# Linear attention with a feed-forward block: `num` bank by bank, and weight preparation, word loads and spills written in another order

## The chip, the cores and the metric

The kernel runs on one core of a Trainium2 chip. The metric is the device time of one execution in microseconds (us). A core has five engines, each of which works strictly in its own written order: PE (TensorE, matmuls and transposes; its weight loads are listed apart as PEld), DVE (VectorE), ACT (ScalarE), POOL (GpSimd) and SP (SyncE, which here issues all the DMAs).

## The reference, cut to what matters

```python
def phi(x):                                  # x: 8 x 8 x 576 x 64, w_phi: 64 x 128
    proj = einsum('bhsd,df->bhsf', x, w_phi)
    proj = proj - max(abs(proj), axis=-1, keepdims=True)
    return concatenate([exp(proj), exp(-proj)], axis=-1)
q_p, k_p = phi(q), phi(k)
kv  = einsum('bhsf,bhsd->bhfd', k_p, v)
z   = sum(k_p, axis=2)
num = einsum('bhsf,bhfd->bhsd', q_p, kv)
den = einsum('bhsf,bhf->bhs', q_p, z)[..., None] + 1e-06
x = (num / den).transpose(0, 2, 1, 3).reshape(4608, 512)
h = x @ w_in                                 # 512 x 2048
g = h * tanh(log1p(exp(h)))
out = g @ w_out                              # 2048 x 512
```

## The kernel before, in words

**Two stages.** The first 280 us or so are the attention stage, all the rest the feed-forward stage (`h` L580, `o` L709 and L732). The feed-forward products run in a split of seven block products, with each fp32 number as a high and a low fp32r part.

**A step of the attention stage.** The 4608 tokens and the heads are cut into 36 units n (NU = 36) of 512 columns. Keys run LEAD = 4 units ahead of queries. In step n PE does, in this order: `dt_n` (L449, sixteen transposes of the centred queries), `pp_k` (L300, projection of the keys of unit n+5), `pp_q` with `xt` (L309 and L315, the next projection of queries, with the transposes of the finished x of the unit before between its matmuls), `num_n` (L340 in `q_num`, 64 matmuls into two PSUM banks i = 0 and 1), `kvps` (L340 in `k_sum`, the product of keys and values), and then `dt_(n+1)`.

**Who waits for whom.** `dt`, `xt`, `num` and `kvps` share four PSUM buffers (pool `ps_b`), which they take in turn. So the second half of `xt` waits until ACT has read the first `dt` bank (`e_q`, exp, L454), the first bank of `num` waits for the exps of the second, the second bank of `num` waits until ACT has copied `xt` (`xs`, L501), and the next `dt` waits until DVE has read the `num` banks (`x`, L482). DVE's work in a step is `m_k` (L331) and `e_k` (L332), `m_q` (L429), `r` (L479), `x` (L482, twice) and `e_q` (L435), all on the step's own data. ACT's is `e_q` (L454, four), `xs` (L501, two), `e_k` (L374, two), `r` (L474, two) and `kv` (L406).

**Weight preparation.** Meanwhile the weights, which arrive as words of 64 bits, are made into their high and low parts, in pieces; 16 of these, called beat pieces, lie in the attention stage, one in two steps. Piece i is counted from 0: pieces 0, 1, 2, 3 are (in,0,0), (in,0,1), (in,1,0), (in,1,1). A piece consists of: the load of its words (SP, L168), `absolute` (ACT, L187), `clamp` (POOL, L190), `shift` (DVE, L194), `sign` (DVE, L198), `scale` (DVE, L204), `low_scale` (POOL, L213), `low` (POOL, L219), `total` (POOL, L231), four `sums` (POOL, L242), `hi` (ACT, CAST, L247), `lo` (POOL, L251), and from piece 4 of the inner matrix on two stores, the spills (SP, L271), of which the second carries what `lo` wrote. Their DVE operations read and write SBUF; those of the step, named above, read PSUM.

**What sets the order.** Every operation is put into one list by `at(time, function)` with a planned time: `base(n)` is the planned start of step n, to which hand-tuned offsets are added (`BEAT_AT` for a beat piece, `LOAD_AT`, `K_AT`, `Q_AT`, `EXP_AT`). The list sorted by time is the written order of all engines. A planned time is only a place in that order; what runs when is decided by the waits.

The constants at the top, BEAT_AT among them, give for a beat piece the offsets of `absolute, clamp, shift, sign, scale, low_scale` from its own step; with that line the diff begins.

Of the kernel before, what the change touches and what calls it, by code (L numbers as in the profile page):

```python
# [27 lines left out]
NU = NTOK * NHP // 512  # L28
# [3 lines left out]
LEAD = 4  # L32
LEAD_STEP = 3.04
L_AT = (0.0, 2.62, 3.19, 7.71, 9.38)
STEP = 7.341
# [3 lines left out]
SPILL_AT = (1.2, 1.9)  # L39
# [7 lines left out]
EXP_AT, MAX_AT = 2.95, 2.5  # L47
# [2 lines left out]
PRE = (11.72, 6.53)  # L50
CONV = (13.41, 14.719)
WORD_AT = 4.79
BEAT_AT = (-5.73, -5.54, -4.04, -4.03, 3.3, 0.5)
BEAT_LOW, BEAT_HI = 3.4, 16.43
X0_AT = (38.06, 20.0)
X0_STORE_AT = (16.4, 16.35, 16.3, 16.25, 16.2, 15.0, 14.9)
# [32 lines left out]
def attention_then_mish(ctx, tc, qT, kT, va, w_phi, w_in, w_out, w_out2, out):  # L89
# [81 lines left out]
    def weight_ops(kind, fp, k, quiet, early):  # L171
# [104 lines left out]
        if early:  # L276
            ops = list(zip(BEAT_AT, (absolute, clamp, shift, sign, scale, low_scale)))
        elif not quiet:
# [57 lines left out]
    def halves(ps, lhsT, rhs, start, stop):  # L336

        for h in range(2):
            rows = slice(h * D, (h + 1) * D)
            nc.tensor.matmul(ps[rows], lhsT[:, rows], rhs[h], start=start, stop=stop, skip_group_check=True)  # L340
# [115 lines left out]
    def q_num(n):  # L456
        c, g = divmod(n, 2)
        es = q_live.pop(n)
        x = x_live[n] = att.tile([P, 2, 2, P], F32, tag="x", name=f"x_{n}", bufs=3)
        for i in range(2):  # L460
            num_live[n, i] = ps_b.tile([P, 2, 2, VW], F32, tag="b", name=f"num{i}_{n}")
        for j in range(2):
            for i in range(2):
                for t in range(2):
                    r0 = (2 * c + t) * P
                    for s in range(2):
                        halves(num_live[n, i][:, t, j], es[:, j, s, (2 * i + t) * P:(2 * i + t + 1) * P],
                               [kv[(r0 + h * D) // S, 2 * g + i][:, j, s] for h in range(2)],
                               start=(t == j == s == 0), stop=(s == 1))
# [363 lines left out]
    def at(time, fn, *args):  # L833
        events.append((time, len(events), fn, args))

    def base(step):
        if step < 0:
            return step * LEAD_STEP
        return min(step, NU - LEAD) * STEP + max(0, step - NU + LEAD) * TAIL_STEP

    for u in range(NU):
        t, after = base(u - LEAD), base(u - LEAD + 1)
        a = K_AT if u >= LEAD else L_AT
        if u < LEAD:
            t = after = base(-LEAD) + u * LEAD_STEP
        at(t + (LOAD_AT[0] if u >= LEAD else -11.1), k_load, u)
        at(t + (LOAD_AT[1] if u > LEAD else V_AT[u]), v_load, u)
        at(t + a[0] - (1.7 if u == LEAD + 1 else 0.0), k_proj, u)
        at(t + a[1], k_center, u)
        if u < LEAD:  # L850
            at(t + a[2], k_exps, u)
        else:
            at(t + EXP_AT, k_exp, u, 1)
            at(t + a[2], k_exp, u, 0)
        at(after + a[3], k_sum, u)
        at(after + a[4], k_store, u)
        t, after, end = base(u), base(u + 1), base(u + 2)
        cut = STEP - TAIL_STEP
        after -= cut if u == NU - LEAD - 1 else 0.0
        close_by = end - (cut if u >= NU - LEAD - 2 else 0.0)  # L860
        if u >= NU - LEAD:
            after = end = close_by = t
        a = T_AT if u >= NU - LEAD else Q_AT
        early = 0.49 if u == 1 else 0.0
        at(t + LOAD_AT[2] - early, q_load, u)
        if 3 <= u <= NU - LEAD:
            at(t + a[0], q_proj_out, u, u - 3)
        else:
            at(t + a[0] - early, q_proj, u)
        if 3 <= u < NU - LEAD:  # L870
            at(t + MAX_AT, q_max, u)
            at(t + a[1], q_sub, u)
        else:
            at(t + a[1] - early, q_center, u)
        for j in range(2):
            at(after + a[2] + 0.45 * j - early, q_turn, u, j)
            shift = (0.0, -0.8)[j] if u == NU - LEAD - 1 else (0.8, 0.0)[j] if u == NU - LEAD else 0.0
            at(after + a[3] + 1.2 * j - early + shift, q_exp, u, j)
        at(end + a[4], q_num, u)
        at(end + a[5], q_den, u)  # L880
        at(end + a[5] + 0.05, q_norm, u)
        if u > NU - LEAD - 3:
            at(close_by + a[6] + (1.78 if u in (NU - LEAD - 2, NU - LEAD - 1) else 0.0), q_out, u)
        at(close_by + a[7] + (0.9 if u == NU - 1 else -0.68 if u == NU - LEAD - 2 else 0.0), q_store, u)
# [26 lines left out]
    def t_of(n):  # L911
        if n > first2:
            m = n - first2
            return t_of(first2) + m * FF2STEP + max(0, (m - 2) // NSEC) * TRAIL
        return begin + 5.6 + (n - AHEAD) * FFSTEP if n >= AHEAD else begin - PRE[0] + PRE[1] * n

    quiet_at = [(3, 0), (4, 0), (6, 0)] + [(n, w) for n in range(9, first2 - 3, 3) for w in (0, 1)]
    quiet_at += [(first2 - 3, 0), (first2 - 3, 2), (first2 - 2, 3)]
    for i, pc in enumerate(pieces):
        quiet = i >= EARLY  # L920
        if quiet:
            n, which = quiet_at[i - EARLY]
            clock = t_of(n) + BITS_AT[which]
            load_at = clock - WORDS_AT
        else:
            clock = CONV[0] + CONV[1] * i - WORD_AT
            load_at = clock + WORD_AT + (LOAD_AT[3] if i else -12.0)
        beat = 2 <= i < EARLY
        bits, sums, high, spill = weight_ops(*pc, quiet, beat)
        if beat:  # L930
            clock = base(2 * i)
            load_at = clock + BEAT_AT[0] - 11.0
        at(load_at, weight_load, *pc)
        for delay, op in bits:
            wait = base(2 * i + 1) + Q_AT[1] + 0.02 if i < 2 and delay > 1.0 else 0.0
            at(max(clock + delay * (0.85 if quiet else 1.0), wait - (0.49 if i == 0 else 0.0)), op)
        clock += LOW_AT[which] if quiet else BEAT_LOW if beat else WORD_AT
        for j, (cost, op) in enumerate(sums):
            if beat:
                clock = base(2 * i) + (BEAT_HI + 0.1 * (j - high) if j >= high else BEAT_LOW + 0.1 * j)  # L940
            at(clock, op)
            if pc[1] >= 2 and j in (high, len(sums) - 1):
                at(clock + (SPILL_AT[j > high and not quiet] if not beat else 1.2 if j == high else 3.2), spill, int(j > high))
            clock += cost

    for s, (sc, fps) in enumerate(segs):
# [7 lines left out]
        t = t_of(n - 2) - XS_EARLY if n >= AHEAD + 2 else begin - X0_AT[s]  # L954
# [12 lines left out]
    for n, (s, sc, fp, first, last) in enumerate(steps):  # L967
        t = t_of(n)
        if second(n):
            a, m = STEP2_AT, n - first2  # L970
# [4 lines left out]
            if n == len(steps) - 1:  # L975
                a = a[:4] + tuple(x - LAST for x in a[4:])
# [23 lines left out]
            if last:  # L1000
                t5, a = t_of(n + 2), DRAIN_AT
# [12 lines left out]
        a = STEP1_AT  # L1014
# [92 lines left out]
```

## Time and profile before

| | us |
|---|---|
| median of 3 runs | 1021.59 (1021.11 to 1024.95) |
| the profiled execution | 1026.97 |
| span of its profile | 1025.2 |
| PE busy | 999.5 (97%) |
| DVE, ACT, POOL busy | 750.0, 505.0, 284.0 |

The profile is of one execution. PE is busy nearly throughout; its share is an average over the two stages, and the rows below take them apart. "Idle before" in a row is the time in which the engine did nothing just ahead of that row, with what ended it; "issue" means that it waited for nothing that the profile shows. PEclk is the granted clock of TensorE, 1.00 being 2.4 GHz and 0.50 the lower level of 1.2 GHz.

### The profile page before, as it was taken

The page shows a single profiled execution, that of the slowest core. Times are in us where ns is not written, and L with a number is a line of the kernel's source. Part 1 is how long each engine was busy: PE and PEld are TensorE (multiplying, and loading weights), DVE is VectorE, ACT ScalarE, POOL GpSimd, SP SyncE. Part 2 cuts the span into 40 slices and gives each one's busy share as a digit, 9 for nine tenths or more (in the row PEclk, how much of TensorE's full clock was granted, in tenths as well). Part 3 has the DMA queues.
Part 4 walks back from the last instruction along what each step waited for, and adds up shares of the span by engine and source line. Part 5 has one row for each costly group of instructions (what it writes and reads, how often), then busy time and mean ns, then how long its engine had stood idle before and what let it go on. Part 6 is the DMA issues. An engine that isn't in the chain of part 4 may idle for free.

```text
span 1025.2 us, 28984 instructions
## 1 busy us (share of the span) xinstructions
PE 999.5 (97%) x12418; PEld 957.4 (93%) x12418; DVE 750.0 (73%) x1168; ACT 505.0 (49%) x904; POOL 284.0 (28%) x267
## 2 busy tenths in 40 slices
PE   8879999999999999999999999999999999999998
PEld 7879988999899999999999999999999999999998
DVE  7769878988755878979886576767676767575755
ACT  5657877877753545544544442423232333333332
POOL 0554354536424314654347001000000001010101
PEclk9989999999999999999999999999999999999999
DMA  6536557776499777898849895959595959585842
GB/s 212 182 127 208 177 172 257 237 249 188 144 355 396 293 275 258 265 362 321 283 156 346 304 359 207 343 190 347 191 355 183 349 195 332 210 315 216 309 162 75
DMA packets 111200, 259.02 MB, mean 253 GB/s; under 512 B 8672, under 2 KB 47328, under 8 KB 109024
## 3 DMA queue, kind: packets, MB, share of 16 engines
q1 hardware_dynamic: 111072, 257.17, 70.9%
q8 instruction: 98, 1.61, 0.6%
q14 instruction: 30, 0.25, 0.1%
HBM read 179.27 MB, written 77.86 MB: 251 GB/s over the span
## 4 chain that ended last, share of the span: by engine, by line
PE 91%; ACT 4%; issue 2%; DMA 1%; POOL 1%; DVE 0%; SPq 0%; ACTq 0%
PE h L580 35%; PE o L732 22%; PE o L709 14%; PE num L340 7%; PE kvps L340 7%; ACT e_q L454 4%; PE dt L449 2%; PE pp_k L300 2%; PE pp_q L309 1%; PE pp_q L300 0%; DMA kraw<-kT 0%; DMA qraw<-qT 0%; DMA v<-va 0%; ACT w_out L187 0%; PE xt L315 0%
## 5 line engine op out<-in xcount | busy, mean ns | idle before, releaser
L580 PE MATMUL h<-xc,win 128*128 128x256 f32 x3024 | 380.4, 283 | 0.0
L580 PEld LDWEIGHTS h<-xc,win 128*128 128x128 f32 x3024 | 373.8, 192 | 4.5
L804 POOL TENSOR_TENSOR part<-part,du 128x512 f32<-128x512 f32 x18 | 23.3, 1293 | 425.7 <-DVE du L794 425.7
L732 PE MATMUL o<-wa,gh 128*128 128x256 f32 x720 | 130.7, 283 | 0.0
L732 PEld LDWEIGHTS o<-wa,gh 128*128 128x128 f32 x720 | 111.8, 192 | 0.0
L709 PE MATMUL o<-wout,gh 128*128 128x512 f32 x432 | 108.2, 392 | 0.0
L732 PE MATMUL o<-wa,gl 128*128 128x256 f32 x360 | 100.7, 283 | 0.0
L612 DVE TENSOR_TENSOR u<-h,u 128x512 f32<-128x512 f32 x72 | 49.5, 687 | 69.3 <-PE h L580 69.3
L732 PE MATMUL o<-wb,held 128*128 128x256 f32 x795 | 95.8, 281 | 0.2 <-DVE du L794 0.2
L732 PEld LDWEIGHTS o<-wb,held 128*128 128x128 f32 x795 | 94.9, 189 | 0.4 <-DVE du L794 0.4
L709 PEld LDWEIGHTS o<-wout,gh 128*128 128x128 f32 x432 | 77.7, 189 | 13.9
L340 PE MATMUL num<-kv,e_q 128*64 128x65 f32 x2304 | 81.2, 226 | 5.7 <-issue 2.2
L340 PEld LDWEIGHTS num<-kv,e_q 128*64 128x64 f32 x2304 | 74.0, 139 | 13.1 <-ACT e_q L454 5.8
L454 ACT ACTIVATE e_q<-dt 128x512 f32<-128x512 f32 x144 | 74.3, 604 | 18.7 <-PE dt L449 18.6
L340 PE MATMUL kvps<-v,e_k 128*64 128x65 f32 (+1 forms) x2560 | 78.6, 224 | 2.5 <-issue 2.5
L340 PEld LDWEIGHTS kvps<-v,e_k 128*64 128x64 f32 (+1 forms) x2560 | 73.5, 138 | 4.7 <-issue 3.0
L628 ACT ACTIVATE sb<-h 128x256 f32<-128x256 f32 x45 | 17.3, 385 | 119.3 <-PE h L580 85.5
L374 ACT ACTIVATE e_k<-e_k 128x1024 f32<-128x1024 f32 x64 | 67.6, 1057 | 14.2 <-DVE e_k L332 14.0
L631 ACT ACTIVATE u<-u 128x768 f32<-128x768 f32 x45 | 38.1, 847 | 72.8 <-DVE u L612 72.8
L667 ACT CAST gh<-sb 128x1024 fp32r<-128x1024 f32 x45 | 47.2, 1049 | 50.4 <-DVE sb L660 50.4
L732 PEld LDWEIGHTS o<-wa,gl 128*128 128x128 f32 x360 | 68.6, 192 | 0.0
L679 DVE TENSOR_TENSOR gl<-sb,gh 128x1024 fp32r<-128x1024 f32 x45 | 61.0, 1355 | 0.7 <-ACT gh L667 0.7
(111 smaller groups left out, 1612.5 us busy)
## 6 DMA issues: line engine op xcount, KB each, us to landing
win<-in_spill SPq DMA_DIRECT2D x44, 896.0 KB, 8.2
xc<-xc_spill SPq DMA_DIRECT2D x63, 512.0 KB, 5.7
xc_spill<-xc SPq DMA_DIRECT2D x56, 512.0 KB, 6.5
wa<-out_spill SPq DMA_DIRECT2D x29, 768.0 KB, 5.8
in_spill<-wst_in SPq DMA_DIRECT2D x24, 448.0 KB, 3.3
v<-va SPq DMA_DIRECT2D x32, 325.0 KB, 4.4
qraw<-qT SPq DMA_DIRECT2D x36, 256.0 KB, 3.6
x_spill<-xs SPq DMA_DIRECT2D x36, 256.0 KB, 2.3
```

The lines of the kernel that those rows point to most:

```text
L300: nc.tensor.matmul(ps[:, j, n], src, w_phi2[rows], start=True, stop=True)
L340: nc.tensor.matmul(ps[rows], lhsT[:, rows], rhs[h], start=start, stop=stop, skip_group_check=True)
L374: nc.scalar.activation(e[:, :, s], e[:, :, 0], AF.Exp, scale=2.0 * s - 1.0)
L454: nc.scalar.activation(e[:, s, h], ps, AF.Exp, scale=2.0 * s - 1.0)
L580: nc.tensor.matmul(ps, w, x, start=(i in (0, 2) and m == 0), stop=(m == 5), skip_group_check=True)
L612: nc.vector.tensor_tensor(u[:, 0:3:2] if second(n) else u[:, 1:3], hy, u2.unsqueeze(1).broadcast_to([P, 2, CH]), op=ALU.add)
L631: nc.scalar.activation(u[:, 0:3], u[:, 0:3], AF.Mish)
L667: nc.scalar.copy(gh, u_live[n][4])
L679: nc.vector.tensor_tensor(gl, u_live[n][4], g_live[n]["h"].bitcast(F32), op=ALU.subtract)
L709: nc.tensor.matmul(o_live[s][tt], g[:, 2 * f + which, cols], wout[fp][:, f, k], start=(first and g is gh and f == k == 0), stop=(last and ...
L732: nc.tensor.matmul(ps, g, w, start=(start and k == 0), stop=(stop and k == 2), skip_group_check=True)
L804: nc.gpsimd.tensor_tensor(cross, cross, d_live[s, tau][0].unsqueeze(1).broadcast_to([P, 2, CH]), op=ALU.add)
```

## The change

It has seven parts.

1. `absolute` of a beat piece gets a place 0.12 later in the plan, by which it stands behind the two `xs` copies of its step on ACT.
2. `q_num` writes all 32 matmuls of bank 0 ahead of the 32 of bank 1; before, the banks took turns of 16.
3. For units 5 to 8 of the keys the two `e_k` exps stand together behind the two `r`; before, one stood ahead of them.
4. In the last unit of the keys, `k_sum` and `k_store` stand ahead of that step's `num` and `r`.
5. The load of a beat piece's words gets a later place on SP, behind the load of `v`.
6. Of piece 2, `shift` and `sign` go one step (7.341) later, and `scale`, `low_scale`, `low`, `total` and `sums` behind those of piece 1.
7. The second spill of a beat piece goes from 3.2 to 5.25 behind its place in the plan, which is behind the loads of `qraw` and `v` on SP.

```diff
-BEAT_AT = (-5.73, -5.54, -4.04, -4.03, 3.3, 0.5)
+BEAT_AT = (-5.61, -5.54, -4.04, -4.03, 3.3, 0.5)
...
-        for j in range(2):
-            for i in range(2):
+        for i in range(2):
+            for j in range(2):
                 for t in range(2):
...
         else:
-            at(t + EXP_AT, k_exp, u, 1)
+            at(t + (EXP_AT if u > LEAD + 4 else a[2]), k_exp, u, 1)
             at(t + a[2], k_exp, u, 0)
-        at(after + a[3], k_sum, u)
-        at(after + a[4], k_store, u)
+        at(after + a[3] - (1.34 if u == NU - 1 else 0.0), k_sum, u)
+        at(after + a[4] - (1.7 if u == NU - 1 else 0.0), k_store, u)
...
+    def bits_of(bits, *which):
+        return [bits[k][1] for k in which]
+
...
             clock = base(2 * i)
-            load_at = clock + BEAT_AT[0] - 11.0
+            load_at = clock - (15.0 if i > 3 else 13.4)
         at(load_at, weight_load, *pc)
         for delay, op in bits:
+            if i == 2 and op in bits_of(bits, 2, 3):
+                delay += STEP
+            if i == 2 and op in bits_of(bits, 4):
+                delay += 0.05
+            if i == 2 and op in bits_of(bits, 5):
+                delay += 6.2
...
-                clock = base(2 * i) + (BEAT_HI + 0.1 * (j - high) if j >= high else BEAT_LOW + 0.1 * j)
+                clock = base(2 * i) + (BEAT_HI + 0.1 * (j - high) if j >= high else BEAT_LOW + 0.1 * j + (3.35 if i == 2 else 0.0))
             at(clock, op)
             if pc[1] >= 2 and j in (high, len(sums) - 1):
-                at(clock + (SPILL_AT[j > high and not quiet] if not beat else 1.2 if j == high else 3.2), spill, int(j > high))
+                at(clock + (SPILL_AT[j > high and not quiet] if not beat else 1.2 if j == high else 5.25), spill, int(j > high))
```

**POOL in steps 1 to 4.** In the rows, `w_in_1` and `t_in_1` with the lower numbers belong to piece 1, `w_in_0` and `t_in_0` to piece 2; `w_in_1_1089` is piece 3. `L213` is `low_scale`, `L219` `low`, `L231` `total`, `L242` `sums`, `L251` `lo`, `L190` `clamp`. Before:

```order
L213 TENSOR_SCALAR w_in_1_736<-words_in_1_585 128x512
L219 TENSOR_TENSOR t_in_1_855<-w_in_1_736,t_in_1_855 128x512
L213 TENSOR_SCALAR w_in_0_757<-words_in_0_548 128x512
L231 TENSOR_TENSOR w_in_1_736<-w_in_1_736,t_in_1_855 128x512
L242 TENSOR_TENSOR w_in_1_736<-w_in_1_736 128x128 x2
L219 TENSOR_TENSOR t_in_0_1014<-w_in_0_757,t_in_0_1014 128x512
L231 TENSOR_TENSOR w_in_0_757<-w_in_0_757,t_in_0_1014 128x512
L242 TENSOR_TENSOR w_in_0_757<-w_in_0_757 128x128 x2
L242 TENSOR_TENSOR w_in_1_736<-w_in_1_736 128x128
L242 TENSOR_TENSOR w_in_0_757<-w_in_0_757 128x128 x2
L242 TENSOR_TENSOR w_in_1_736<-w_in_1_736 128x128
L251 TENSOR_TENSOR win_697<-w_in_1_736,win_697 128x896
```

After:

```order
L213 TENSOR_SCALAR w_in_1_736<-words_in_1_583 128x512
L219 TENSOR_TENSOR t_in_1_853<-w_in_1_736,t_in_1_853 128x512
L231 TENSOR_TENSOR w_in_1_736<-w_in_1_736,t_in_1_853 128x512
L242 TENSOR_TENSOR w_in_1_736<-w_in_1_736 128x128 x4
L251 TENSOR_TENSOR win_697<-w_in_1_736,win_697 128x896
L213 TENSOR_SCALAR w_in_0_761<-words_in_0_586 128x512
L219 TENSOR_TENSOR t_in_0_1012<-w_in_0_761,t_in_0_1012 128x512
L231 TENSOR_TENSOR w_in_0_761<-w_in_0_761,t_in_0_1012 128x512
L242 TENSOR_TENSOR w_in_0_761<-w_in_0_761 128x128 x4
L190 TENSOR_SCALAR w_in_1_1089<-w_in_1_1089 128x512
L213 TENSOR_SCALAR w_in_1_1089<-words_in_1_893 128x512
L251 TENSOR_TENSOR win_1242<-w_in_0_761,win_1242 128x896
```

Piece 1 is finished, `lo` included, before piece 2's `low_scale` begins, and piece 3's `clamp` and `low_scale` come right behind piece 2's sums.

**DVE in steps 1 to 3.** `L194` is `shift`, `L198` `sign`, `L204` `scale`; the other lines are the step's own. Before:

```order
L194 TENSOR_SCALAR w_in_1_736<-w_in_1_736 128x512
L194 TENSOR_SCALAR w_in_0_757<-w_in_0_757 128x512
L198 SCALAR_TENSOR_TENSOR w_in_0_757<-words_in_0_548,w_in_0_757 128x512
L198 SCALAR_TENSOR_TENSOR w_in_1_736<-words_in_1_585,w_in_1_736 128x512
L204 TENSOR_SCALAR t_in_1_855<-w_in_1_736 128x512
L331 TENSOR_REDUCE m_k_957<-pp_k_883 128x8
L332 TENSOR_TENSOR e_k_956<-pp_k_883,m_k_957 128x2x512
L429 TENSOR_REDUCE m_q_961<-pp_q_900 128x8
L479 RECIPROCAL r_964<-r_964 128x8
L482 TENSOR_TENSOR x_921<-num_2_922,r_964 128x256
L482 TENSOR_TENSOR x_921<-num_2_923,r_964 128x256
L435 TENSOR_TENSOR e_q_1012<-pp_q_900,m_q_961 128x2x512
```

After, from piece 1's `scale` on:

```order
L204 TENSOR_SCALAR t_in_1_853<-w_in_1_736 128x512
L331 TENSOR_REDUCE m_k_954<-pp_k_879 128x8
L332 TENSOR_TENSOR e_k_953<-pp_k_879,m_k_954 128x2x512
L429 TENSOR_REDUCE m_q_958<-pp_q_897 128x8
L479 RECIPROCAL r_960<-r_960 128x8
L482 TENSOR_TENSOR x_918<-num_2_919,r_960 128x256
L482 TENSOR_TENSOR x_918<-num_2_920,r_960 128x256
L435 TENSOR_TENSOR e_q_1008<-pp_q_897,m_q_958 128x2x512
L194 TENSOR_SCALAR w_in_0_761<-w_in_0_761 128x512
L198 SCALAR_TENSOR_TENSOR w_in_0_761<-words_in_0_586,w_in_0_761 128x512
L204 TENSOR_SCALAR t_in_0_1012<-w_in_0_761 128x512
```

Piece 2's `shift` and `sign` have left the place ahead of piece 1's `scale` and stand one step later, between `e_q` and the next `m_k`, with piece 2's `scale`, which stood there before, behind them.

**ACT in step 1**, from the exps of `dt_1` to the copy of `kv`. Before:

```order
L187 ACTIVATE w_in_1_736<-words_in_1_585 128x512
L187 ACTIVATE w_in_0_757<-words_in_0_548 128x512
L501 COPY xs_759<-xt_0_738 128x4x64
L501 COPY xs_759<-xt_0_739 128x4x64
L374 ACTIVATE e_k_799<-e_k_799 128x2x512
L474 ACTIVATE r_807<-num_1_765 128x4
L474 ACTIVATE r_807<-num_1_766 128x4
```

After:

```order
L187 ACTIVATE w_in_1_736<-words_in_1_583 128x512
L501 COPY xs_757<-xt_0_738 128x4x64
L501 COPY xs_757<-xt_0_739 128x4x64
L187 ACTIVATE w_in_0_761<-words_in_0_586 128x512
L474 ACTIVATE r_806<-num_1_765 128x4
L474 ACTIVATE r_806<-num_1_766 128x4
L374 ACTIVATE e_k_799<-e_k_799 128x2x512 x2
```

Piece 2's `absolute` went behind the `xs` copies, and the first `e_k` exp went behind the two `r`.

## Rows read from the trace of the kernel before

**Rows 1.** Windows: us, then busy us of PE, PEld, DVE, ACT, POOL; PEclk, DMA share, GB/s

```profile
40.00:60.00 20.00, 13.40 (x364) 12.67 (x364) 15.53 (x22) 9.76 (x21) 13.40 (x17) 0.94 0.38 124
...
280.00:300.00 20.00, 20.00 (x225) 18.55 (x222) 10.02 (x19) 11.76 (x23) 7.08 (x6) 1.00 0.88 323
```

**Rows 2.** Waits of PE: who waited for what, us in total, times, longest

```profile
PE xt L315 <- ACT e_q L454: 6.8, 2, 5.9
...
PE num L340 <- ACT xs L501: 0.7, 2, 0.6
```

**Rows 3.** PE, timeline: start, us, engine, line, operation, count [idle before]

```profile
39.01 0.69 PE L340 MATMUL num<-kv,e_q 128*64 128x65 f32 x16
...
43.70 0.71 PE L449 MATMUL dt<-ident,e_q 64*128 64x64 f32 x16
...
51.33 1.01 PE L449 MATMUL dt<-ident,e_q 64*128 64x64 f32 x16 [0.62 <-DVE x L482]
...
60.39 0.69 PE L315 MATMUL xt<-ident,x 64*128 64x64 f32 x4 [5.94 <-ACT e_q L454]
61.36 3.63 PE L340 MATMUL num<-kv,e_q 128*64 128x65 f32 x64 [0.29 <-ACT e_q L454]
...
66.80 0.71 PE L449 MATMUL dt<-ident,e_q 64*128 64x64 f32 x16
...
69.57 2.09 PE L340 MATMUL num<-kv,e_q 128*64 128x65 f32 x64
...
73.45 0.71 PE L449 MATMUL dt<-ident,e_q 64*128 64x64 f32 x16
```

**Rows 4.** ACT, timeline, the stretch of PE's longest wait

```profile
58.41 0.94 ACT L247 CAST win<-w_in 128x896 fp32r<-128x896 f32 x1 [6.77 <-POOL w_in L242]
```

**Rows 5.** POOL, timeline, pieces 1 to 3

```profile
46.96 1.28 POOL L219 TENSOR_TENSOR t_in<-w_in,t_in 128x512 f32<-128x512 f32 x1 [4.09 <-DVE t_in L204]
48.33 1.55 POOL L213 TENSOR_SCALAR w_in<-words_in 128x512 f32<-128x512 uint32 x1
...
53.06 1.27 POOL L219 TENSOR_TENSOR t_in<-w_in,t_in 128x512 f32<-128x512 f32 x1 [0.76 <-DVE t_in L204]
54.41 1.26 POOL L231 TENSOR_TENSOR w_in<-w_in,t_in 128x512 f32<-128x512 f32 x1
55.75 2.63 POOL L242 TENSOR_TENSOR w_in<-w_in 128x128 f32<-128x128 f32 x6
59.43 2.08 POOL L251 TENSOR_TENSOR win<-w_in,win 128x896 fp32r<-128x896 f32 x1 [1.05 <-ACT win L247]
62.30 0.61 POOL L190 TENSOR_SCALAR w_in<-w_in 128x512 f32<-128x512 f32 x1 [0.79 <-ACT w_in L187]
```

**Rows 6.** DVE, timeline, pieces 1 to 3 between the step's own work

```profile
46.39 0.43 DVE L204 TENSOR_SCALAR t_in<-w_in 128x512 uint32<-128x512 uint32 x1
...
52.56 0.42 DVE L204 TENSOR_SCALAR t_in<-w_in 128x512 uint32<-128x512 uint32 x1
...
67.37 0.42 DVE L194 TENSOR_SCALAR w_in<-w_in 128x512 uint32<-128x512 uint32 x1
...
68.50 1.23 DVE L331 TENSOR_REDUCE m_k<-pp_k 128x8 f32<-128x1024 f32 x1
...
72.55 0.76 DVE L482 TENSOR_TENSOR x<-num,r 128x256 f32<-128x256 f32 x2
```

**Rows 7.** Feed-forward stage: the same DVE line beside a POOL operation and alone

```profile
334.84 2.43 POOL L251 TENSOR_TENSOR wst_in<-w_in,wst_in 128x896 fp32r<-128x896 f32 x1 [1.06 <-ACT wst_in L247]
335.20 3.16 DVE L649 TENSOR_TENSOR gl<-u,gh 128x1024 fp32r<-128x1024 f32 x1
...
344.99 1.22 DVE L649 TENSOR_TENSOR gl<-u,gh 128x1024 fp32r<-128x1024 f32 x1
```

**Rows 8.** PE, timeline: a gap without a releaser, and the last unit's step

```profile
128.99 0.92 PE L340 MATMUL num<-kv,e_q 128*64 128x65 f32 x24 [1.02 <-issue]
...
260.08 2.09 PE L340 MATMUL num<-kv,e_q 128*64 128x65 f32 x64 [0.52 <-ACT e_q L454]
```

## Prediction

> **What bounds the kernel now.** I read the windows of the whole span first, then the waits of PE, then the timelines of PE, ACT, POOL and DVE around its longest wait. The windows [rows 1] show PE busy for 20.00 of 20 us from 280 us on: the feed-forward stage has no slack, and nothing in the change touches its work. A gain can only come from the attention stage, where the worst window, 40 to 60 us, has 13.40 us of PE. The waits of PE [rows 2] put 5.9 of its 6.6 idle us down to one wait, `xt` for the exps `e_q` of step 3. It ends at 60.39, and the step that holds it, from `dt_3` at 51.33 to `dt_4` at 66.80, lasts 15.47 us, where the next, to `dt_5` at 73.45, takes 6.65 [rows 3]. So 8.8 us are lost in that step.
>
> The exps are not to blame. In ACT's timeline [rows 4] CAST `hi` of weight piece 1 starts at 58.41 after 6.77 us idle for POOL's `sums`, so ACT was ready at 51.64; the exps stand behind it. On POOL [rows 5] pieces 1 and 2 take turns from 46.96 to 58.38: `low_scale` of piece 2 (1.55), its `low` (1.27, which itself waits for DVE), its `total` and half of the six last `sums` lie ahead of piece 1's last sum. This interleaving is the bound of that step.
>
> **Part by part.** I follow the time of `dt` from step to step; what is gained at `dt_5` stays, since after it both orders have the same work to do.
>
> *`num` bank by bank, and `absolute` behind `xs`.* In step 1 `num` and `kvps` take 43.70 − 39.01 = 4.69; without a wait they take 73.45 − 69.57 = 3.88 [rows 3]. The difference, 0.81, is the wait of bank 1 for the `xs` copy [rows 2], which stood behind piece 2's `absolute` on ACT, and came due after 16 matmuls where now 32 lie ahead. I take all of it: `dt_2` at 42.89. The second wait of this kind (0.7 in all, 0.6 the longest) [rows 2] leaves 0.15 for later.
>
> *Piece 2 behind piece 1, up to the CAST.* On DVE, `shift` and `sign` of piece 2 leave the place ahead of piece 1's `scale`. The pair costs 68.50 − 67.37 = 1.13 [rows 6]. So `scale` comes at 46.39 − 1.13 = 45.26 at the latest (earlier by up to 0.5, as `num_1` ends sooner). `low` follows 0.57 behind (46.39 to 46.96) [rows 5, 6], then `total` 1.35 later, the sums 1.34 later, and four of the six sums, 1.75: done by 50.27 [rows 5]. `dt_3` loses its wait for `x` (0.62, since DVE is 1.13 and more ahead) and the 0.81: 51.33 − 1.43 = 49.90. ACT, as far ahead, gets to the CAST at 51.64 − 1.43 = 50.21. The wait of 6.77 is gone, at most 0.05 is left.
>
> *What is late next.* The second half of `xt` comes 1.98 behind the CAST, and `num_3` 2.95 behind it (60.39 and 61.36 after 58.41): 53.16. With 3.88 for `num` and `kvps`, PE could start `dt_4` at 57.04. But now piece 2's `shift`, `sign` and `scale` stand together on DVE in this step, where piece 2's `scale` stood alone: 52.56 − 1.43 = 51.13 [rows 6]. `lo` of piece 1 starts on POOL at 50.21 + 1.02 = 51.23 and takes 2.08 [rows 5]. The feed-forward stage shows what such a meeting does [rows 7]: L649, an operation of DVE with its inputs in SBUF, takes 1.22 alone and 3.16 when it starts 0.36 after `lo`; it ends 1.09 after `lo` does. It was held until `lo` ended. So `sign` of piece 2 is held to about 53.6 (`shift` got in ahead and delays `lo` by some 0.3), and then `low_scale` (1.55), next on POOL, comes between it and the end of `scale`. Depending on who goes first, `scale` ends between 54.7 and 56.3; I take 55.95, near the end where POOL goes first. The next `m_k` starts then, the `x` comes 72.55 − 68.50 = 4.05 behind it [rows 6], and a `dt` that waits for the two `x` some 0.57 behind that (an estimate: three quarters of their 0.76): `dt_4` at 55.95 + 4.62 = 60.57. PE idles 3.5 us there, less than the 5.94 before.
>
> Step 4 has the same once more. `low` of piece 2 starts at 56.1, `total` and `sums` end at 56.1 + 1.35 + 1.34 + 1.75 = 60.55, and only then comes `clamp` of piece 3 (0.61, from 60.6), with `low_scale` (1.55) up to 62.85. Piece 3's `shift` is due on DVE at 61.8, meets that `low_scale` and is held to 62.85; with 1.13 for the pair, `m_k` is at 64.0, and `dt_5` 4.62 later, **68.6**, where it was 73.45. This part's gain, with that of `num_1`, is **4.85**.
>
> *The last unit.* `num_32` waits 0.52 for exps [rows 8], and `kvps` will fill that. The copy of `kv` then stands ahead of the last `r` on ACT, which is worth between −0.7 and +0.5; I take the upper end, **0.5**, as PE is the later of the two there.
>
> *`e_k` in two units* goes behind `r`; the keys are four units ahead, which hides it: 0, and a few tenths at most if `kv` comes late. *Word loads and second spills* go behind the loads of `v` and `qraw`; no wait of PE on such a load after the start is among its waits, so 0. Since no row shows them at their new places, I bound this by the gaps without a releaser: one such gap is 1.02 [rows 8], so −1.0 to +1.0 is kept for one more or one fewer.
>
> *The slower clock.* `num_3` ran at 3.63 instead of 2.09 behind the long stall [rows 3], at the lower of the two levels. After a shorter stall I expect such a stretch again, but mostly covered by DVE's lateness in step 4; 0.2 is taken off.
>
> The sum is 4.85 + 0.15 + 0.5 − 0.2 = **5.3 us**. It is made against the profiled execution (1026.97, its span 1025.2), which is 5.4 longer than the median; the stretches used here have no gap without a releaser in them, so I subtract it from the median: 1021.59 − 5.3 = **1016.3**.
>
> **A rule that speaks against the change.** The meeting in [rows 7] is that of one operation, a TENSOR_TENSOR; no row of the trace has `sign` beside a POOL operation. The Trainium skill, "SBUF — State Buffer", section "Who interferes with whom", states that VectorE and GpSimd share a port pair which is an exclusive lock, that a VectorE instruction with two SBUF inputs contends with a GpSimd one that reads SBUF, and that the order of issue decides who blocks. By this rule `sign` is held like L649, the trace agrees for L649 with 3.16 against 1.22, and the sum is 5.3; without it, it would be the 8.1 of the first rival.
>
> **Rivals.**
>
> *DVE is not held* (POOL alone is late). Then `sign` and `scale` of piece 2 end by 52.7 and `dt_4` comes at 57.04. POOL: `lo` to 53.3, `low_scale` to 54.85, `low`, `total`, `sums` to 59.35, `clamp` of piece 3 to 60.05; `shift` of piece 3 waits for it, `m_k` at 61.2, `dt_5` at 65.8. The gain there is 7.65, in all 8.1: **1013.5**. For it: `sign` is another form than that in [rows 7]. Against it: [rows 7].
>
> *The stall goes and nothing takes its place.* `dt_5` at 57.04 + 6.65 = 63.7, a gain of 9.75, in all 10.2: **1011.4**. Against it: piece 3's `clamp` stands behind all of piece 2's sums, and DVE behind that.
>
> *Less comes through.* The low clock is not covered (3.63 − 2.09 = 1.54), and piece 4's `shift` also meets a `low_scale` (up to 1.0): 5.3 − 2.6 = 2.7, **1018.9**. For it: the stall of 3.5 us that I forecast is still long.
>
> *Slower: the queue.* With 14 word loads now directly behind loads of `v`, and second spills behind those, the transfers come in a bunch, and each bunch could bring a gap like that at 128.99, where PE stood for 1.02 and waited for nothing shown [rows 8]. Fourteen of them are 14.3, against 5.3 gained: **1030.6**. It decides the sign from 5.3 / 14 = 0.38 each. Against it: in the feed-forward window [rows 1] the DMA share is 0.88 and PE is never idle.
>
> **How the numbers follow.** The forecast has 0.50 (1014.5 to 1017.7 by the bounds of `scale` and of the last unit), DVE not held 0.17, nothing in its place 0.08, less comes through 0.19, slower 0.06. The range of 8 in 10 goes from 1012.0, which leaves out most of the cleanest case, to 1019.6, which leaves out the slower case and the end of the one before. A measurement of this kernel can tell about 0.5%, 5.1 us, from no change: the bound is 1016.5, so just over half of the forecast (0.28) and the two better cases are faster, 0.53; the rest of the forecast and the smaller gain are the same, 0.41; slower 0.06.
>
> **What would show it.** In the changed trace: no wait of bank 1 of `num_1`; CAST `hi` of piece 1 at about 50.2 without a wait; `dt_3` at 49.9; L198 of piece 2 at some 51.5, taking 2.8 rather than 0.69; PE waiting for `x` at `dt_4` until 60.6; POOL's `clamp` of piece 3 at 60.6; `dt_5` at 68.6. Wrong would be: L198 at 0.69 beside `lo`, which gives the first rival; the CAST still waiting for `sums`; or new gaps without a releaser behind word loads, which gives the last.

## The result, and the profile after

The changed kernel takes 1010.35 us (median of 4 runs, 1008.41 to 1011.75), the kernel before 1022.49 (4 runs, 1021.11 to 1024.95): the ratio is 0.9877, with a 95% interval of 0.985 to 0.9904. It is faster, as forecast, but by 12.1 us instead of 5.3, and lies below the range. That it lies next to the rival in which the stall goes and nothing takes its place (1011.4) does not make that rival right: PE waits 1.09 and 1.27 us for `x` in the rows below. The profiled execution took 1010.88, its span is 1009.1.

PE's windows of the changed kernel (columns as in [rows 1]): the window of 40 to 60 us has 18.34 us of PE instead of 13.40, and the feed-forward stage is as full as before.

```profile
40.00:60.00 20.00, 18.34 (x500) 17.60 (x498) 18.55 (x24) 15.84 (x33) 15.81 (x18) 1.00 0.57 184
...
280.00:300.00 20.00, 20.00 (x136) 18.53 (x135) 11.56 (x20) 11.03 (x20) 0.00 (x0) 1.00 1.01 380
```

Its waits of PE, to be read against [rows 2]: the 5.9 us wait of `xt` and those for `xs` are gone, and `dt` now waits for `x`. "Issue" marks what is called a gap without a releaser below.

```profile
PE dt L449 <- DVE x L482: 2.8, 3, 1.3
PE kvps L340 <- issue: 2.1, 3, 1.1
...
PE num L340 <- ACT e_q L454: 0.9, 3, 0.5
```

PE's timeline, against [rows 3], from `num_1` to `dt_6`:

```profile
36.13 2.09 PE L340 MATMUL num<-kv,e_q 128*64 128x65 f32 x64 [0.20 <-ACT e_q L454]
...
40.02 0.71 PE L449 MATMUL dt<-ident,e_q 64*128 64x64 f32 x16
...
46.96 0.71 PE L449 MATMUL dt<-ident,e_q 64*128 64x64 f32 x16
...
50.37 2.09 PE L340 MATMUL num<-kv,e_q 128*64 128x65 f32 x64 [0.52 <-ACT e_q L454]
...
55.62 0.68 PE L449 MATMUL dt<-ident,e_q 64*128 64x64 f32 x15 [1.09 <-DVE x L482]
...
63.76 0.68 PE L449 MATMUL dt<-ident,e_q 64*128 64x64 f32 x15 [1.27 <-DVE x L482]
...
70.65 0.71 PE L449 MATMUL dt<-ident,e_q 64*128 64x64 f32 x16
```

ACT, POOL and DVE of the changed kernel, against [rows 4], [rows 5] and [rows 6]: CAST of piece 1 starts at 47.42 without a wait; `lo` of piece 1 runs from 48.43 to 50.81; DVE's `shift` and `sign` of piece 2 (47.73, 48.18) come through ahead of it, and `scale` (48.98) takes 2.13 instead of 0.42 and ends 0.30 after `lo`.

```profile
47.42 0.94 ACT L247 CAST win<-w_in 128x896 fp32r<-128x896 f32 x1
```

```profile
48.43 2.38 POOL L251 TENSOR_TENSOR win<-w_in,win 128x896 fp32r<-128x896 f32 x1 [1.55 <-ACT win L247]
50.90 1.62 POOL L213 TENSOR_SCALAR w_in<-words_in 128x512 f32<-128x512 uint32 x1
...
57.10 0.62 POOL L190 TENSOR_SCALAR w_in<-w_in 128x512 f32<-128x512 f32 x1
57.80 1.78 POOL L213 TENSOR_SCALAR w_in<-words_in 128x512 f32<-128x512 uint32 x1
```

```profile
47.73 0.42 DVE L194 TENSOR_SCALAR w_in<-w_in 128x512 uint32<-128x512 uint32 x1
48.18 0.69 DVE L198 SCALAR_TENSOR_TENSOR w_in<-words_in,w_in 128x512 uint32<-128x512 uint32 x1
48.98 2.13 DVE L204 TENSOR_SCALAR t_in<-w_in 128x512 uint32<-128x512 uint32 x1
51.02 1.21 DVE L331 TENSOR_REDUCE m_k<-pp_k 128x8 f32<-128x1024 f32 x1
...
57.75 0.43 DVE L194 TENSOR_SCALAR w_in<-w_in 128x512 uint32<-128x512 uint32 x1 [0.81 <-POOL w_in L190]
58.21 1.03 DVE L198 SCALAR_TENSOR_TENSOR w_in<-words_in,w_in 128x512 uint32<-128x512 uint32 x1
59.17 1.21 DVE L331 TENSOR_REDUCE m_k<-pp_k 128x8 f32<-128x1024 f32 x1
```

So steps 1 to 5 went by the mechanism that was forecast, at a lower price. They took 70.65 − 32.73 = 37.9 us from `dt_1` to `dt_6`, against 80.77 − 35.57 = 45.2 before: 7.3 of the 12.1. The rest had to lie elsewhere, and two things offered themselves. The gaps of PE without a releaser sum to 7.4 us in the waits of before and to 3.9 after. And the odd steps from 7 on are shorter: where nothing disturbs them, 7.30 us from one `dt` to the next before and 6.94 after, while the even ones are 6.79 in both. In step 7 of before, `num` is one row without an idle time, but 2.45 us long; in the changed kernel it is 2.09. The idle time stands with the weight loads of the same matmuls (PEld), as the second row shows, and the list of waits of before has it there too (third row); in the list of the changed kernel no such line is left:

```profile
90.78 2.45 PE L340 MATMUL num<-kv,e_q 128*64 128x65 f32 x64
```

```profile
91.60 1.48 PEld L340 LDWEIGHTS num<-kv,e_q 128*64 128x64 f32 x48 [0.28 <-ACT xs L501]
```

```profile
PEld num L340 <- ACT xs L501: 2.3, 7, 0.7
```

The changed kernel in its step 7:

```profile
80.34 2.09 PE L340 MATMUL num<-kv,e_q 128*64 128x65 f32 x64
```

On ACT in that step of before, `absolute` and then the `xs` copies stand just where `num` is under way:

```profile
90.59 0.70 ACT L187 ACTIVATE w_out<-words_out 128x512 f32<-128x512 f32 x1
91.15 0.68 ACT L501 COPY xs<-xt 128x256 f32<-128x256 f32 x2
```

One correction to the section on the kernel: the offsets of `BEAT_AT` hold for fourteen pieces, 2 to 15; pieces 0 and 1 have places of their own, so part 1 of the change moves `absolute` in the odd steps of pieces 2 to 15.

### The profile page after: what moved, and what is told of

It is laid out like the page before. It is cut to its first block, busy times and chain, and to the rows that moved or that the text cites. A ratio compares the mean times of both kernels' runs of the same rounds, so it can differ in the third digit from the quotient of the medians.

```text
span 1009.1 us, 28988 instructions
## 1 busy us (share of the span) xinstructions
PE 992.0 (98%) x12418; PEld 952.1 (94%) x12418; DVE 751.3 (74%) x1168; ACT 504.4 (50%) x904; POOL 286.0 (28%) x267
## 4 chain that ended last, share of the span: by engine, by line
PE 91%; ACT 5%; issue 2%; POOL 1%; DVE 1%; DMA 0%; SPq 0%; DVEq 0%
PE h L580 36%; PE o L732 22%; PE o L709 15%; PE num L340 7%; PE kvps L340 6%; ACT e_q L454 3%; PE dt L449 2%; PE pp_k L300 1%; PE pp_q L309 1%; ACT e_k L374 1%; DMA kraw<-kT 0%; PE pp_q L300 0%; PE xt L491 0%; DVE e_k L332 0%; PE xt L315 0%
## 5 line engine op out<-in xcount | busy, mean ns | idle before, releaser
L804 POOL TENSOR_TENSOR part<-part,du 128x512 f32<-128x512 f32 x18 | 23.4, 1297 | 425.8 <-DVE du L794 425.8
L340 PEld LDWEIGHTS num<-kv,e_q 128*64 128x64 f32 x2304 | 71.0, 137 | 8.6 <-ACT e_q L454 5.8
L340 PE MATMUL num<-kv,e_q 128*64 128x65 f32 x2304 | 76.2, 223 | 2.9 <-issue 0.9
L374 ACT ACTIVATE e_k<-e_k 128x1024 f32<-128x1024 f32 x64 | 67.7, 1057 | 11.5 <-DVE e_k L332 11.1
```

Source lines behind the costliest of these rows:

```text
L374: nc.scalar.activation(e[:, :, s], e[:, :, 0], AF.Exp, scale=2.0 * s - 1.0)
L804: nc.gpsimd.tensor_tensor(cross, cross, d_live[s, tau][0].unsqueeze(1).broadcast_to([P, 2, CH]), op=ALU.add)
```

## The experiments

The theories first. For steps 1 to 5 there was one, that of the prediction, with a hold of DVE by POOL to be tested. For the other 5 us: **A**, the word loads and spills at their new places (parts 5 and 7) leave fewer gaps; **B**, the gaps are an affair of the single execution; and, once the odd steps had been seen, that the `xs` wait costs 0.35 us in each of them and parts 1 and 2 end it.

**1. The changed kernel again, and again.** No edit.

> The changed kernel again, for its scatter and a second profile. In the first profile dt_0 to dt_5 took 36.3 us where the kernel before took 47.8, and the gaps of PE without a releaser (issue) fell from 7.4 to 3.9 us. Theory A (the shorter steps 1 to 5 give 7 to 8 us, and the new places of word loads and second spills on SP give the other 4 to 5 by fewer such gaps): gaps near 3.9 again. Theory B (the gaps differ from one execution to the next and have nothing to do with SP's order): gaps anywhere from 3 to 8. Both: about 12 us faster than the kernel before, dt_0 to dt_5 within 1 us of 36.3 apart from gaps.

Measured: 1013.74 us, ratio 0.9899 (0.9874 to 0.9925). Beside the last three experiments it ran once more.

> The changed kernel once more, so that the next three have it beside them on the same chip. From dt_1 to dt_6 37.8 to 37.9 us as in its first two profiles, where the kernel before takes 45.2; num 2.09 in all odd steps from 5 on; 10 to 12 us faster than the kernel before. The gaps without a releaser at other places than in the first two profiles.

Measured: 1012.83 us, ratio 0.9895 (0.9871 to 0.9919). Steps 1 to 5 are 37.9, 37.8 and 37.9 us in its three profiles; the gaps without a releaser sum to 3.9, 3.9 and 5.8 and lie only in part at the same places (of those of 0.3 us or more, one stands in step 19 in all three, and no other step has one in all three). The gain is 10 to 12 us, with the first measurement at the upper end.

**2. SP's order undone, and alone.** The changed kernel without part 7, and without part 5 from piece 4 on; and the kernel before with only these.

```diff
-            load_at = clock - (15.0 if i > 3 else 13.4)
+            load_at = clock - (16.73 if i > 3 else 13.4)
...
-                at(clock + (SPILL_AT[j > high and not quiet] if not beat else 1.2 if j == high else 5.25), spill, int(j > high))
+                at(clock + (SPILL_AT[j > high and not quiet] if not beat else 1.2 if j == high else 3.2), spill, int(j > high))
```

> The changed kernel with part 7 undone, and part 5 undone for the pieces from 4 on: only SP's order differs from the changed kernel. Theory A: 4 to 5 us slower than the changed kernel run beside it, with more gaps without a releaser. Theory B: within 1.5 us of it.

Measured: 1013.18 us, ratio 0.9893 (0.9868 to 0.9919), beside 1013.74 of the changed kernel on the same chip; gaps 3.5.

> The kernel before with only part 7, and part 5 for the pieces from 4 on: only SP's order differs from the kernel before. Theory A: 4 to 5 us faster than the kernel before. Theory B: within 1.5 us of it.

Measured: 1021.44 us, ratio 0.9978 (0.9957 to 0.9999); gaps 4.8 in its profile, 45.2 us from `dt_1` to `dt_6`. In the changed kernel these parts give nothing; on the kernel before the interval leaves between 0.1 and 4.4 us, so a small gain there is not excluded. Theory A's 4 to 5 us fall in the changed kernel (runs of 1011.9 to 1014.5 without these parts, 1013.0 to 1014.8 with them); on the kernel before the interval only just reaches 4.

**3. Part 6 alone**, with part 5 for pieces 2 and 3 along with it; no run has these two apart.

```diff
+            if i == 2 and op in bits_of(bits, 2, 3):
+                delay += STEP
+            if i == 2 and op in bits_of(bits, 4):
+                delay += 0.05
+            if i == 2 and op in bits_of(bits, 5):
+                delay += 6.2
...
-                clock = base(2 * i) + (BEAT_HI + 0.1 * (j - high) if j >= high else BEAT_LOW + 0.1 * j)
+                clock = base(2 * i) + (BEAT_HI + 0.1 * (j - high) if j >= high else BEAT_LOW + 0.1 * j + (3.35 if i == 2 else 0.0))
```

> The kernel before with only part 6 (and part 5 for pieces 1 to 3, whose word buffers part 6 needs early): DVE and POOL have the order of the changed kernel, PE that of before. Theory A and B by steps: dt_1 to dt_5 as much shorter as in the changed kernel less the 0.8 of num_1, so 6.5 us faster in all and the CAST of piece 1 without its wait of 6.77; no less than 4 and no more than 8.5. Were it 10 or more, the other parts would be worth nothing.

Measured: 1017.34 us, ratio 0.9933 (0.9913 to 0.9953), that is 6.9 us faster, close to the 6.5 expected; 39.0 us from `dt_1` to `dt_6`, 6.2 less than before. On ACT the CAST comes without a wait, and `dt_4` waits for `x` as in the changed kernel:

```profile
48.69 0.94 ACT L247 CAST win<-w_in 128x896 fp32r<-128x896 f32 x1
```

```profile
37.95 1.62 PE L340 MATMUL num<-kv,e_q 128*64 128x65 f32 x48 [0.69 <-ACT xs L501]
...
52.83 1.62 PE L340 MATMUL num<-kv,e_q 128*64 128x65 f32 x48 [0.50 <-ACT xs L501]
...
57.64 0.68 PE L449 MATMUL dt<-ident,e_q 64*128 64x64 f32 x15 [1.12 <-DVE x L482]
```

The waits of the second `num` bank for `xs` are still there, 0.69 in step 1 and 0.50 in step 3.

In this kernel `sign` of piece 2 starts 0.04 after `lo` of piece 1 and is held, 2.60 us instead of 0.69, ending 0.56 after `lo`. `scale` then runs within `low_scale` of piece 2 and takes 0.68 instead of 0.43, so it is not held to the end of `low_scale`. From `shift` to `m_k` it takes 53.04 − 49.29 = 3.75 us. DVE and POOL:

```profile
49.29 0.42 DVE L194 TENSOR_SCALAR w_in<-w_in 128x512 uint32<-128x512 uint32 x1
49.74 2.60 DVE L198 SCALAR_TENSOR_TENSOR w_in<-words_in,w_in 128x512 uint32<-128x512 uint32 x1
52.44 0.68 DVE L204 TENSOR_SCALAR t_in<-w_in 128x512 uint32<-128x512 uint32 x1
53.04 1.21 DVE L331 TENSOR_REDUCE m_k<-pp_k 128x8 f32<-128x1024 f32 x1
```

```profile
49.70 2.08 POOL L251 TENSOR_TENSOR win<-w_in,win 128x896 fp32r<-128x896 f32 x1 [1.47 <-ACT win L247]
51.87 1.84 POOL L213 TENSOR_SCALAR w_in<-words_in 128x512 f32<-128x512 uint32 x1
```

**4. Parts 1 and 2, each alone and together**, on the kernel before. From here on, theory A in the expectations is that the `xs` wait lengthens `num` in the odd steps, and theory B that the order of the banks itself does.

```diff
-BEAT_AT = (-5.73, -5.54, -4.04, -4.03, 3.3, 0.5)
+BEAT_AT = (-5.61, -5.54, -4.04, -4.03, 3.3, 0.5)
```

> The kernel before with only part 1: absolute of the pieces from 2 on behind the xs copies on ACT; PE keeps its order of banks. Theory A: in the odd steps from 5 to 27 the second bank of num waits for xs, which shows only as a num of 2.44 to 2.46 us instead of 2.09 from its first matmul to its last, some ten times 0.35; the copies coming 0.6 us sooner are enough to end it. Then num takes 2.09 in all those steps and the kernel is 3.5 to 4.5 us faster than before. Theory B: the longer num comes from the order of the banks itself and not from xs: num stays at 2.44 and the kernel within 1 us of before, but for the 0.6 of num_1.

Measured: 1020.98 us, ratio 0.9990 (0.9977 to 1.0003), an interval that includes no change.

```diff
-        for j in range(2):
-            for i in range(2):
+        for i in range(2):
+            for j in range(2):
```

> The kernel before with only part 2: num bank by bank on PE, nothing else moved. Theory A: the second bank is needed some 0.96 us later, which covers the 0.35 by which xs is late: num at 2.09 in the odd steps, 3.5 to 4.5 us faster than before, the same as part 1 alone. Theory B: the same gain, but from the order alone, so that part 1 alone gives nothing. Both: the wait of 5.94 in step 3 stays.

Measured: 1020.73 us, ratio 0.9982 (0.9968 to 0.9997). In both, `num` takes 2.08 or 2.09 in the odd steps, as in these two rows of step 7, part 1 alone and part 2 alone:

```profile
88.84 2.09 PE L340 MATMUL num<-kv,e_q 128*64 128x65 f32 x64
```

```profile
87.04 2.08 PE L340 MATMUL num<-kv,e_q 128*64 128x65 f32 x64
```

So the long `num` was the wait for `xs`, and either part ends it; the rival that it lies in the order of the banks falls. But the time came out below what was expected, 1.5 to 1.7 us by the medians.

> The kernel before with parts 1 and 2 together. Each of them alone brought num to 2.09 in the odd steps, and 1.5 to 1.7 us by the medians. Theory A: both remove the same wait, so together no more than either alone: 1 to 3 us faster than before. Rival D (they add up): 3 to 4 us faster.

Measured: 1022.52 us against 1024.30, ratio 0.9976 (0.9957 to 0.9996), 2.5 us by the ratio. By the time alone rival D is not excluded (0.4 to 4.4 us); against it stands that either part alone already brings `num` to 2.09 in all odd steps from 5 on. Why less than ten times 0.35: in the four profiles with neither part, the excess of `num` over 2.09 in the odd steps from 5 to 27 sums to 2.0 (the kernel before), 3.3 (parts 5 and 7), 2.4 (part 6) and 3.4 us (the changed kernel without parts 1 and 2, below). Some odd steps have no excess: `num` takes 2.08 to 2.15 in steps 13 and 15 in all four. Why the wait stays out there is not shown.

**5. Parts 1 and 2 undone, part 6 undone.**

> The changed kernel with parts 1 and 2 undone. Theory A: num back at 2.44 in the odd steps and longer in steps 1 and 3: 4 to 5.5 us slower than the changed kernel, that is 6 to 7.5 us faster than the kernel before, like part 6 alone. Rival: the gain of part 6 alone (6.5 us) and that of parts 1 and 2 overlap, and this kernel is within 2 us of the changed one.

Measured: 1014.75 us, ratio 0.9924 (0.9907 to 0.9940); `num` back at 2.44 to 2.46 in nine odd steps, and at 3.00 and 2.94 in steps 1 and 3. It is 7.8 us faster than before, where 6 to 7.5 were expected. Against the 10 to 12 of the changed kernel that is 2 to 4 us less; as the changed kernel did not run beside it, the rival (within 2 us of it) is not excluded by the time.

> The changed kernel with part 6 undone (and part 5 for pieces 1 to 3): POOL and DVE in the order of before. Theory A (the parts add up; parts 1 and 2 give 0.65 in step 1 and 0.35 in each odd step in which no gap hides it): the wait of 5.94 is back, dt_1 to dt_6 near 44.5, num 2.09 in the odd steps, 2 to 4 us faster than the kernel before and 6.5 to 8.5 slower than the changed one. Rival C (parts 1 and 2 pay only when the long stall is gone): within 1 us of the kernel before.

Measured: 1018.69 us, ratio 0.9956 (0.9937 to 0.9974), 4.5 us faster than before by the ratio, a little more than the 2 to 4 expected, and 5.9 slower than the changed kernel beside it (1012.83); PE's long wait is back, in full:

```profile
58.08 0.69 PE L315 MATMUL xt<-ident,x 64*128 64x64 f32 x4 [5.94 <-ACT e_q L454]
59.06 3.73 PE L340 MATMUL num<-kv,e_q 128*64 128x65 f32 x64 [0.28 <-ACT e_q L454]
```

Part 6 alone gives 0.67%, all without part 6 0.44%: together 1.11%, which is what the changed kernel has beside it (1.05%). The two add up within their intervals (0.2% each way); the rival that parts 1 and 2 pay only without the stall falls.

**6. DVE out of POOL's way.** In the changed kernel, `lo` of piece 1 goes behind `low` of piece 2 on POOL, `absolute` of piece 3 behind the two `r` on ACT (its `shift` and `sign` go later by the same 1.8), and `clamp` of piece 3 ahead of piece 2's sums.

```diff
+            if i == 3 and op in bits_of(bits, 0, 1, 2, 3):
+                delay += 1.8
...
-                clock = base(2 * i) + (BEAT_HI + 0.1 * (j - high) if j >= high else BEAT_LOW + 0.1 * j + (3.35 if i == 2 else 0.0))
-            at(clock, op)
+                clock = base(2 * i) + (BEAT_HI + 0.1 * (j - high) if j >= high else BEAT_LOW + 0.1 * j + (3.35 + (4.4 if j > 1 else 0.0) if i == 2 else 0.0))
+            at(clock + ((0 if j == high else 0.2) if i == 1 and j >= high else 0.0), op)
```

> The changed kernel with lo of piece 1 behind low of piece 2 on POOL, so that it no longer runs beside sign and scale of piece 2 on DVE; absolute of piece 3 behind the r of its step on ACT; clamp of piece 3 ahead of piece 2's sums. If DVE is held by POOL's lo: scale of piece 2 takes 0.42 instead of 2.13, m_k starts 1.0 to 1.1 us sooner, the wait of 1.09 at dt_4 goes, that of 1.27 at dt_5 too or nearly, and the kernel is 1.5 to 2.3 us faster than the changed one. If DVE is not held by it, scale keeps some 2 us and dt_4 its wait, and the kernel is within 0.5 us of the changed one.

Measured: 1009.09 us, ratio 0.9870 (0.9855 to 0.9886), with no changed kernel beside it. `scale` of piece 2 takes 0.43, `m_k` follows at 49.95 (2.36 after `dt_3`, where it came 4.06 after it), and `dt_4` and `dt_5` have no wait: `dt_1` to `dt_6` takes 35.1 us, 2.8 less than in the changed kernel. DVE's and PE's timelines:

```profile
48.36 0.42 DVE L194 TENSOR_SCALAR w_in<-w_in 128x512 uint32<-128x512 uint32 x1
48.81 0.69 DVE L198 SCALAR_TENSOR_TENSOR w_in<-words_in,w_in 128x512 uint32<-128x512 uint32 x1
49.61 0.43 DVE L204 TENSOR_SCALAR t_in<-w_in 128x512 uint32<-128x512 uint32 x1
49.95 1.22 DVE L331 TENSOR_REDUCE m_k<-pp_k 128x8 f32<-128x1024 f32 x1
```

```profile
54.89 0.71 PE L449 MATMUL dt<-ident,e_q 64*128 64x64 f32 x16
...
61.55 0.71 PE L449 MATMUL dt<-ident,e_q 64*128 64x64 f32 x16
```

> The changed kernel with lo of piece 1 out of the way of DVE, again, now beside the changed one. In its first profile dt_1 to dt_6 took 35.1 us where the changed kernel takes 37.9. If this carries through to the end: 2 to 3 us faster than the changed kernel beside it (0.997 to 0.998 of it). If the gaps without a releaser that follow take it back: within 1 us.

Measured: 1011.33 us, ratio 0.9877 (0.9855 to 0.9899), beside 1012.83 of the changed kernel: 1.5 us by the medians, between the two forecasts and less than the two intervals can tell apart. So the shorter steps are shown, and a gain in the whole time is not. Its profile shows where a gain of this size can go. The steps are short again (36.3 us, of which 0.88 is a gap), but from `dt_12` to `dt_30` this execution took 133.7 us where the first profile of the very same program took 130.1, and its gaps without a releaser sum to 11.1 us against 5.0. The largest of these waits, here and in the first profile of this program:

```profile
PE num L340 <- issue: 4.3, 3, 2.1
PE kvps L340 <- issue: 3.6, 5, 1.2
...
PE pp_k L300 <- issue: 3.2, 4, 1.2
```

```profile
PE kvps L340 <- issue: 2.4, 2, 1.8
PE pp_k L300 <- issue: 1.8, 2, 1.0
...
PE num L340 <- issue: 0.8, 2, 0.5
```

This is theory B at work: one program, two executions, 6 us of gaps apart.

**All profiles side by side**, in us between the first transposes of `dt` (from PE's timelines), with the gaps without a releaser (from the waits). Rows of `dt` are counted; one of them, behind `dt_30`, holds two units. What lies ahead of `dt_1` takes 32.0 to 35.6 us, the most in the kernel before, which has a gap of 2.07 there; what follows `dt_34` lies between 744.1 and 744.9 in all of them.

| kernel | 1 to 6 | 6 to 12 | 12 to 30 | 30 to 34 | gaps | ratio to before |
|---|---|---|---|---|---|---|
| before | 45.2 | 42.9 | 133.5 | 23.7 | 7.4 | 1 |
| parts 5, 7 | 45.2 | 42.2 | 131.4 | 24.3 | 4.8 | 0.9978 |
| part 1 | 44.4 | 41.7 | 133.0 | 24.8 | 9.0 | 0.9990 |
| part 2 | 45.1 | 43.7 | 130.3 | 23.2 | 3.9 | 0.9982 |
| parts 1, 2 | 44.2 | 41.4 | 132.2 | 23.2 | 6.6 | 0.9976 |
| all but 6 | 44.4 | 41.2 | 128.6 | 24.4 | 3.9 | 0.9956 |
| part 6 | 39.0 | 42.3 | 133.0 | 23.7 | 6.6 | 0.9933 |
| all but 1, 2 | 39.1 | 42.3 | 129.3 | 23.6 | 4.1 | 0.9924 |
| all but 5, 7 | 37.9 | 41.9 | 130.2 | 24.3 | 3.5 | 0.9893 |
| changed | 37.9 | 41.5 | 129.0 | 23.8 | 3.9 | 0.9877 |
| changed, second | 37.8 | 41.2 | 129.7 | 23.8 | 3.9 | 0.9899 |
| changed, third | 37.9 | 41.2 | 131.7 | 23.4 | 5.8 | 0.9895 |
| experiment 6 | 35.1 | 41.2 | 130.1 | 23.5 | 5.0 | 0.9870 |
| experiment 6, second | 36.3 | 41.2 | 133.7 | 23.9 | 11.1 | 0.9877 |

The first column is set by part 6, then by parts 1 and 2, and is the same for the same orders within a few tenths, gaps apart. Part 3 shows nothing in it: 44.2 without (parts 1, 2) and 44.4 with it (all but 6), 39.0 without (part 6) and 39.1 with it (all but 1, 2). The second shows the odd steps (three of them: 42.2 or more with the wait, 41.2 without, unless a gap falls in). The third is where the gaps fall, and there single executions scatter by 5 us.

## Why the prediction was wrong

By its own steps:

- **`num` bank by bank and `absolute`, in step 1: right.** Forecast 0.81, measured 8.13 − 7.29 = 0.84.
- **The CAST and its wait: right.** Forecast that ACT gets there with at most 0.05 of waiting; it started at 47.42 without any. Steps 1 and 2 were forecast 0.81 and 0.62 shorter and became 0.84 and 0.69 shorter.
- **What is late next: the right mechanism, too high a price.** DVE was held by POOL's `lo`, and PE waited for `x` at `dt_4` and `dt_5`. But from `shift` of piece 2 to `m_k` it took 51.02 − 47.73 = 3.29 us, not 4.82. The step that failed is "I take 55.95, near the end where POOL goes first": I let `low_scale` of piece 2 come between `lo` and the end of `scale`, and put `sign` on the held side too. `sign` got in ahead of `lo` by 0.25, and only `scale` was held: DVE was earlier against POOL than forecast, with `shift` 0.70 ahead of `lo` (47.73 and 48.43) instead of 0.10 (51.13 and 51.23). In part 6 alone `sign` was held as forecast (2.60 against 2.8), and still it took 3.75, because `scale` ran within `low_scale`. So about 1.07 of the missing 1.53 lies in `low_scale`, which does not hold `scale`, and 0.46 in `sign`. What lets `sign` in ahead is not shown: it does so in the changed kernel without parts 1 and 2 and in the one without parts 5 and 7 too, which leaves part 3 of the parts that touch these steps; this rests on one profile of part 6 alone. In step 4, `shift` of piece 3 was not held by `low_scale`, and `sign` took 0.34 more (1.03 instead of 0.69); `m_k` came 2.07 after the start of `clamp`, not 3.4. The 4.62 from `m_k` to the `dt` that waits for `x` was right (4.60 and 4.59). From `dt_3` to `dt_6` I had 25.9 us (29.44 before, less 3.57: the 4.85 and 0.15 of the sum, of which 1.43 lay ahead of `dt_3`); it took 23.7. This term was mis-sized by 2.2 us, and with it 7.3 instead of 5.0 came out of steps 1 to 5. Experiment 6 shows the hold itself: with `lo` out of the way `scale` takes 0.43 and both waits for `x` are gone.
- **"The second wait of this kind leaves 0.15 for later": wrong.** This is the larger failure by its kind. I read the `xs` waits off PE's lines in the list of waits, which have 0.7 us in all [rows 2]. The wait came back in most odd steps as a `num` of 2.45 us without any idle time in the row, and the excess sums to 2.0 to 3.4 us. The trace of before shows it: PEld's line in the same list has 2.3 us in 7 waits, and the length of one row over the steps (2.09 and 2.45), or the step from `dt` to `dt` in odd and even steps, shows it as well. Parts 1 and 2 together measured 2.5 us (0.4 to 4.4) on the kernel before.
- **The last unit, 0.5: no gain shows.** The stretch that it touches, from `dt_30` to `dt_34`, is 23.7 us in the profile before and 23.8, 23.8 and 23.4 in the three of the changed kernel. Over all fourteen profiles it scatters from 23.2 to 24.8, and the two lowest have no part 4, so a few tenths either way cannot be told; no run has part 4 by itself. The wait of 0.52 for exps went, and `dt` waits 0.48 for `x` instead: `kvps` now runs ahead of `num` on PE, and ACT's last `r` waits for that later `num` (0.76 us), not for the `kv` copy that I had named.
- **The clock, −0.2: not there.** No stretch at the lower level followed the shorter waits (the granted clock of the window above is 1.00, where it was 0.94); `num_3` took 2.09.
- **Loads and spills, 0: held in the changed kernel** (1013.18 without them, 1013.74 with), and the slower rival with gaps behind every bunch did not come. On the kernel before they measured 0.1 to 4.4 us, which stays open.

With 7.3 for steps 1 to 5 and 2 to 3 for the odd steps the sum is 9 to 10.5 instead of 5.3. The measured 10 to 12 in three comparisons leaves up to 3 us that no run assigns; the gaps of single executions differ by more than that, and parts 3 and 4 were not run by themselves.

On the rule that I set against the change: the Trainium skill, "SBUF — State Buffer", section "Who interferes with whom", says that the one who holds the shared ports of VectorE and GpSimd blocks the other fully. For `scale` beside `lo` the trace agrees (2.13 instead of 0.42, to 0.30 after the end of `lo`), and for `sign` beside `lo` in part 6 alone (2.60 instead of 0.69). Beside `low_scale` it does not: in experiment 6 `low_scale` of piece 2 runs from 47.60 to 49.23 (1.63 instead of 1.55), and `shift` at 48.36 takes its usual 0.42 within it, and `sign`, which starts within it at 48.81, its usual 0.69:

```profile
47.60 1.63 POOL L213 TENSOR_SCALAR w_in<-words_in 128x512 f32<-128x512 uint32 x1
50.18 1.27 POOL L219 TENSOR_TENSOR t_in<-w_in,t_in 128x512 f32<-128x512 f32 x1 [0.94 <-DVE t_in L204]
51.41 2.11 POOL L251 TENSOR_TENSOR win<-w_in,win 128x896 fp32r<-128x896 f32 x1
```

I had taken the hold that rows show for `lo` [rows 7] and applied it to `low_scale` as well, which no row supported.

## What to carry to other kernels

A short wait of the matmuls may be listed with their weight loads only (PEld 2.3 us here, PE 0.7); read both, and compare the length of the same row, and of the whole step, between steps of different kinds before you take the listed waits for all there are. When an engine's order is untangled, look up for each meeting of two engines which pair of operations it is, since what one pair shows (`scale` or `sign` beside `lo`) need not hold for another (`shift` beside `low_scale`). And where single executions differ by gaps of several us, judge a change of two or three us by the stretch that it touches, over several profiles, not by the total alone.

## What had not been expected of the hardware

- The gaps of PE without a releaser sum to between 3.5 and 11.1 us in fourteen profiles, and to 5.0 and 11.1 in two executions of one program; they fall mostly between 120 and 250 us, and they differ as much between these two as between any two kernels here.
- A DVE `TENSOR_SCALAR` of 0.42 us was held 1.7 us by POOL's `TENSOR_TENSOR` of 128x896, and a `SCALAR_TENSOR_TENSOR` of 0.69 by 1.9, while POOL's `TENSOR_SCALAR` of 128x512 from uint32 held `shift` and `sign` by nothing in one execution, `sign` by 0.34 in another, in which it took 1.78 itself instead of 1.55, and `scale` by 0.25 in a third, in which it took 1.84.
